# Attention in 24-query blocks with exact maxima, its output kept transposed in SBUF, and a list scheduler in the source

## The chip, the core and the metric

The kernel runs on one core of a Trainium2 chip. Five engines work side by side, each through its own instructions in order: TensorE (PE; its weight loads are listed as PEld), VectorE (DVE), ScalarE (ACT), GpSimd (POOL) and SyncE (SP, which only issues transfers here). Transfers between DRAM and SBUF run on 16 DMA engines; they are issued from SP, ACT or POOL. PE writes into PSUM, eight banks of 128 x 512 float32. The metric is the device time of one execution in microseconds (us), the median of three runs.

## What is computed

For 8 batches of 8 heads, 576 positions, head size 64, two attentions are added. The first pools q, k and v by four along the sequence (144 positions), does a full softmax attention and repeats each output row four times. The second lets each position see only the positions less than four away. The sum, with heads side by side, is a 4608 x 512 input to a gated feed-forward network (FFN) with 1536 inner columns.

```python
factor = 4; Sd = S // factor; scale = 1.0 / np.sqrt(D)
out_up = np.repeat(sm_attn(q_d, k_d, v_d), factor, axis=2)   # q_d, k_d, v_d: means of four
mask = np.abs(pos[:, None] - pos[None, :]) < factor
scores = np.where(mask, scale * np.matmul(q, k.transpose(0, 1, 3, 2)), -1000000000.0)
attn = softmax(scores)                                       # with the row maximum subtracted
attn_out = out_up + np.matmul(attn, v)
x = attn_out.transpose(0, 2, 1, 3).reshape(B * S, H * D)     # 4608 x 512
out = (np.maximum(x @ w_gate, 0.0) * (x @ w_val)) @ w_out    # 512 -> 1536 -> 512
```

## The kernel before

The attention works on 32 pairs of heads (`hp`), four pairs to a batch. The FFN works on nine chunks of 512 tokens; a chunk needs whole batches, since a batch has 576 tokens and all eight heads of it make up the 512 columns of x.

For a pair, `emit_load` brings q and k (96 partitions, six blocks of 96 queries) and windows of v (128 partitions: 96 rows with three before and 29 behind them) into SBUF, all issued from SP. `emit_mid` casts them to float16. `emit_mid_b` transposes q and k on PE against an identity (`tp_ps`, L319), copies them out of PSUM (qT on ACT L328, kT on DVE L330) and pools them by four with two reductions on DVE (L336, L342). `emit_compute` then does the downsampled scores (`sd_ps`, L366), pools v by a matmul with a constant (`vd_ps`, L377), computes band scores in blocks of 96 queries against 128 keys (`sc_ps`, L405), takes exponentials on ACT without subtracting a maximum (L389, L415), multiplies the band by a 0/1 mask on DVE (L418), and sums up: `od_ps` (L429) is the downsampled output with the denominators in a 65th column, `u_ps` (L463) the band output, likewise; `f_ps` (L475) repeats the normalised downsampled output four times by a matmul with a constant. DVE normalises and adds into `x_b` (L484 to L492). Each pair's part of x is written to a DRAM scratch `x_dr` (L503), and transposing loads (L153) bring it back as the `xT` tiles that the FFN needs.

The FFN of a chunk is 12 tasks `ffn_task_h` (L170 and L175: four matmuls each for gate and value, relu on ACT L180, product on DVE L182) and four tasks `ffn_task_y` (12 matmuls each, L191, copied out by ACT L195 and stored). The order is written by hand: the list `sched` gives each pair two slots, and chunk c starts in slot 8c + 11, that is, in the second slot of pair 5 for chunk 0, two tasks to a slot; what has no slot left comes after the last pair (`tail`). Weights arrive in float32 from the ACT queue into staging tiles (L140) and are cast on ACT (L145). Tile pools decide where instructions wait for buffers; PSUM tiles of every kind share the eight banks.

```python
slot = 8 * c + 11
for i, t in enumerate(tasks):
    s = slot + i // 2
    if s < 2 * NP:
        sched[s // 2][s % 2].append(t)
    else:
        tail.append(t)
```

## Time and profile before

| | us |
|---|---|
| median of the three timed runs | 441.45 |
| lowest and highest of them | 439.75, 442.13 |
| span of the profiled execution, first to last instruction | 440.1 |
| PE busy in it | 397.4 |
| DVE busy | 298.4 |
| ACT busy | 211.4 |
| POOL busy | 7.7 |

The profiled execution's time is known by its span alone. A row of the timeline or of the chain of waits starts with the start and the duration in us; matmuls are pipelined, so that their cost is read from start to start and not from the duration. In the groups, `x32 | 23.7, 740` means 32 instructions, 23.7 us busy in all, 740 ns of one; what follows the second bar is idle time of the engine ahead of them and what ended it. `SPq` and `ACTq` are the issuing queues.

### The profile page before, as it was taken

The page shows a single profiled execution, that of the slowest core. Times are in us where ns is not written, and L with a number is a line of the kernel's source. Part 1 is how long each engine was busy: PE and PEld are TensorE (multiplying, and loading weights), DVE is VectorE, ACT ScalarE, POOL GpSimd, SP SyncE. Part 2 cuts the span into 40 slices and gives each one's busy share as a digit, 9 for nine tenths or more (in the row PEclk, how much of TensorE's full clock was granted, in tenths as well). Part 3 has the DMA queues.
Part 4 walks back from the last instruction along what each step waited for, and adds up shares of the span by engine and source line. Part 5 has one row for each costly group of instructions (what it writes and reads, how often), then busy time and mean ns, then how long its engine had stood idle before and what let it go on. Part 6 is the DMA issues. An engine that isn't in the chain of part 4 may idle for free.

```text
span 440.1 us, 9037 instructions
## 1 busy us (share of the span) xinstructions
PE 397.4 (90%) x3408; PEld 227.6 (52%) x3408; DVE 298.4 (68%) x812; ACT 211.4 (48%) x485; POOL 7.7 (2%) x100
## 2 busy tenths in 40 slices
PE   0037778999999999999999999999999999999996
PEld 0026675555555555555565556555655654444442
DVE  0229998998789878977997799779966860330430
ACT  2435876564565455545564556445633532332331
POOL 0000000000000000000000000000000000000000
PEclk9999999999999999999999999999999999999999
DMA  8799989457777787577775646321123112200202
GB/s 288 245 311 224 278 226 243 107 114 174 188 185 172 166 207 176 135 165 215 173 162 132 191 105 138 76 105 33 30 36 109 27 39 48 97 0 9 87 0 95
DMA packets 171730, 60.64 MB, mean 138 GB/s; under 512 B 164264, under 2 KB 164520, under 8 KB 171688
## 3 DMA queue, kind: packets, MB, share of 16 engines
q1 hardware_dynamic: 164008, 41.21, 42.5%
q10 hardware_dynamic: 7680, 18.88, 11.4%
q8 instruction: 26, 0.43, 0.4%
q14 instruction: 16, 0.13, 0.1%
HBM read 41.20 MB, written 14.16 MB: 126 GB/s over the span
## 4 chain that ended last, share of the span: by engine, by line
PE 82%; DMA 7%; DVE 6%; SPq 3%; issue 1%; ACT 1%; DVEq 0%
PE h_ps L170 21%; PE h_ps L175 21%; PE y_ps L191 19%; PE tp_ps L319 3%; PE f_ps L475 3%; PE od_ps L429 3%; PE u_ps L463 3%; DMA vst<-in_v_dram 3%; PE vd_ps L377 3%; PE sc_ps L405 2%; DMA nat<-in_k_dram 2%; SPq L292 2%; PE sd_ps L366 1%; DMA out_dram<-y_sb 1%; DMA masks_sb<-band_masks 1%; SPq L261 1%
## 5 line engine op out<-in xcount | busy, mean ns | idle before, releaser
L170 PE MATMUL h_ps<-xT,wg_sb 128*128 128x512 f16 x432 | 112.1, 382 | 0.0
L175 PE MATMUL h_ps<-xT,wv_sb 128*128 128x512 f16 x432 | 111.7, 381 | 0.0
L191 PE MATMUL y_ps<-wo_sb,gT 128*128 128x512 f16 x432 | 95.7, 379 | 0.0
L175 PEld LDWEIGHTS <-wv_sb 128*128 128x128 f16 x432 | 42.5, 98 | 51.6 <-issue 1.1
L191 PEld LDWEIGHTS <-gT 128*128 128x128 f16 x432 | 41.5, 98 | 48.2
L170 PEld LDWEIGHTS <-wg_sb 128*128 128x128 f16 x432 | 40.3, 99 | 42.3 <-issue 1.6
L195 ACT COPY y_sb<-y_ps 128x512 f32<-128x512 f32 x36 | 21.1, 586 | 78.8 <-PE y_ps L191 72.8
L415 ACT ACTIVATE e_sb<-sc_ps 128x288 f16<-128x288 f32 x128 | 42.0, 416 | 1.1 <-PE sc_ps L405 1.1
L418 DVE TENSOR_TENSOR e_sb<-e_sb,masks_sb 128x288 f16<-128x288 f16 x128 | 36.3, 301 | 4.9 <-ACT e_sb L415 4.9
L463 PEld LDWEIGHTS <-e_sb 128*96 128x96 f16 x384 | 24.8, 138 | 12.0 <-DVE e_sb L418 6.5
L463 PE MATMUL u_ps<-vwin,e_sb 128*96 128x65 f16 x384 | 25.3, 220 | 6.2 <-DVE e_sb L418 6.2
L389 ACT ACTIVATE e_d<-sd_ps 72x288 f16<-72x288 f32 x64 | 22.5, 402 | 16.9 <-PE sd_ps L366 16.8
L394 DVE CAST vd_sb<-vd_ps 72x130 f16<-72x130 f32 x64 | 15.6, 284 | 20.4 <-PE vd_ps L377 20.4
L330 DVE CAST kT<-tp_ps 128x288 f16<-128x288 f32 x64 | 26.7, 442 | 1.5 <-PE tp_ps L319 1.5
L475 PE MATMUL f_ps<-odn,E_sb 72*96 72x64 f16 x384 | 25.6, 220 | 0.0
L429 PE MATMUL od_ps<-vd_sb,e_d 72*72 72x65 f16 x256 | 18.4, 206 | 7.8 <-DVE vd_sb L394 5.9
L328 ACT CAST qT<-tp_ps 128x288 f16<-128x288 f32 x64 | 23.5, 431 | 0.8 <-PE tp_ps L319 0.5
L342 DVE TENSOR_REDUCE k_dT<-kT 128x144 f16<-128x576 f16 x32 | 23.7, 740 | 0.0
L336 DVE TENSOR_REDUCE q_dT<-qT 128x144 f16<-128x576 f16 x32 | 23.6, 739 | 0.0
L475 PEld LDWEIGHTS <-E_sb 72*96 72x96 f16 x384 | 22.8, 138 | 0.0
L307 DVE CAST vwin<-vst 128x768 f16<-128x768 f32 x32 | 17.7, 553 | 6.5 <-DMA vst<-in_v_dram 6.5
L429 PEld LDWEIGHTS <-e_d 72*72 72x72 f16 x256 | 16.9, 123 | 10.0 <-issue 3.8
(556 smaller groups left out, 452.9 us busy)
## 6 DMA issues: line engine op xcount, KB each, us to landing
vst<-in_v_dram SPq DMA_DIRECT2D x62, 192.0 KB
nat<-in_q_dram SPq DMA_DIRECT2D x32, 288.0 KB
nat<-in_k_dram SPq DMA_DIRECT2D x32, 288.0 KB
out_dram<-y_sb ACTq DMA_DIRECT2D x8, 1024.0 KB
x_dr<-x_b SPq DMA_DIRECT2D x32, 144.0 KB
wstage<-in_moe_w_gate_dram ACTq DMA_DIRECT2D x4, 768.0 KB
wstage<-in_moe_w_val_dram ACTq DMA_DIRECT2D x4, 768.0 KB
wstage<-in_moe_w_out_dram ACTq DMA_DIRECT2D x12, 256.0 KB
```

The costliest lines, as they stand in the source:

```text
L170: nc.tensor.matmul(out=h1, lhsT=wg_sb[:, kk, bass.ts(jj, 128)], rhs=xts[kk], start=(kk == 0), stop=(kk == 3),)
L175: nc.tensor.matmul(out=h2, lhsT=wv_sb[:, kk, bass.ts(jj, 128)], rhs=xts[kk], start=(kk == 0), stop=(kk == 3),)
L191: nc.tensor.matmul(out=y_ps, lhsT=st["gts"][jj][:, bass.ts(ty, 128)], rhs=wo_sb[:, jj, :], start=(jj == 0), stop=(jj == NJJ - 1),)
L328: nc.scalar.copy(out=o, in_=tp)
L330: nc.vector.tensor_copy(out=o, in_=tp)
L336: nc.vector.tensor_reduce(out=q_dT, in_=qT[:, KPAD : KPAD + S].rearrange("p (t f) -> p t f", f=4), axis=mybir.AxisListType.X, op=ALU.add,)
L342: nc.vector.tensor_reduce(out=k_dT, in_=kT[:, KPAD : KPAD + S].rearrange("p (t f) -> p t f", f=4), axis=mybir.AxisListType.X, op=ALU.add,)
L415: nc.scalar.activation(out=esb, in_=scps[hh][:, :, 0:NQ], func=AF.Exp, scale=scale)
L418: nc.vector.tensor_tensor(out=esb, in0=esb, in1=masks_sb[:, 3 * g2 : 3 * g2 + 3, :], op=ALU.mult,)
L429: nc.tensor.matmul(out=od_ps[0:72, hh, tcx, :], lhsT=ed_sb[hh][:, c, bass.ts(tcx, 72)], rhs=vd_sb[hh][:, c, :], start=(c == 0), stop=(c == 1),
L463: nc.tensor.matmul(out=up[:, j, :], lhsT=e_sb[hh][j // 3][:, j % 3, :], rhs=vw[:, hh, j, :], start=True, stop=True,)
L475: nc.tensor.matmul(out=fp[:, j, :], lhsT=E_sb[0:72, j % 3, :], rhs=odn_sb[hh][0:72, j // 3, :], start=True, stop=True,)
```

## The change

The attention is written anew, the FFN keeps its matmuls, and the whole program is put in order by a planner in the source: every piece of work is an `Op` with an engine (or several to choose from), an assumed duration, the ops it depends on and a priority; `list_schedule` simulates five in-order engines, takes at each step the op that can start first (among those within 0.05 us, the one of the lowest priority number), and the instructions are emitted in that order. Attention has lower numbers than the FFN. PSUM's banks are split, four for the FFN and four for attention.

For a pair, q and k come as nine tiles of 128 rows with both heads side by side (`nat`), are cast (`c16`), and nine PE transposes (T) give q and k of both heads as one `qkT`. One reduction pools both by four (`qkd`). The scores (S) are computed with queries on the partitions: 24 blocks of 24 queries against 32 keys for each of two heads, 48 matmuls with 32-column weights of 64 rows, and 12 matmuls of 24 downsampled queries against 144 keys. DVE adds a mask of 0 and -1e30, takes row maxima, subtracts them, and after the exponential on ACT sums, inverts and normalises; the downsampled maxima go by POOL (scaled by `nb`) into the bias of three exponentials on ACT. The band weights are transposed in 32 x 32 blocks on DVE (`at2`), the downsampled ones on PE (W, six transposes) and copied by ACT. V multiplies: 12 matmuls for the band, 4 for the downsampled part, with the output transposed (head columns on the partitions). v is loaded twice, as windows (`vw32`) and in groups of four rows (`v4`) that are added up by POOL or DVE. Two additions on DVE write the sum, downsampled columns repeated by the access pattern, straight into `xT` in SBUF; the DRAM scratch, its writes and transposing loads, the staging tiles and casts of the weights are gone. The weights are loaded by POOL's queue with the cast to float16 done by the transfer. Stores of y go from SP, one for each 128 tokens.

```diff
-    sched = [[[], []] for _ in range(NP)]
...
-            vd = a_vd.tile([72, 2, 65], FP16, name="vd_sb", tag="vd_sb")
...
-        nc.sync.dma_start(
-            _dap(
-                x_dr,
...
+    def start_of(o, eng):
+        t = max(avail[eng], data_at(o, eng))
+        if o.need:
+            name, n = o.need
+            p = pools[name]
+            if len(p) < n:
+                return None
+            t = max(t, sorted(p)[n - 1][0] + SEM)
+        return t
+
...
+        best = None
+        starts = {}
+        ends = {}
+        for e, rs in ready.items():
+            for o, dur in rs:
+                s = start_of(o, e)
+                if s is None:
+                    continue
+                starts[o.seq, e] = s
+                ends[o.seq] = min(ends.get(o.seq, (1e9, "")), (s + dur, e))
+        for (i, e), s in starts.items():
+            if ends[i][1] == e and (best is None or s < best[0]):
+                best = (s, e)
+        assert best is not None, "the graph is stuck"
+        t0, e = best
+        o, dur = min(((o, d) for o, d in ready[e]
+                      if starts.get((o.seq, e), 1e9) <= t0 + eps[e] and ends[o.seq][1] == e),
+                     key=lambda x: (x[0].prio, x[0].seq))
...
+    for g in range(4):
+        for nm, dst, src in (("g", wg_sb, moe_w_gate), ("v", wv_sb, moe_w_val)):
+            w_ld[nm, g] = add(POOL, 1.2, wpiece(dst, src, 384 * g, 384, 0), prio=-40 + g,
+                              xfer=2.2, after=6.0 + 5.0 * g)
+    for g in range(4):
+        w_ld["o", g] = add(POOL, 1.2, wopiece(3 * g, 3), prio=-30 + g, xfer=2.2,
+                           after=28.0 + 3.0 * g)
...
+        r["cast"] = cast = add_any(
+            copies(c_, nt_, (POOL, 1.15), (DVE, 0.77), (ACT, 1.2)),
+            [lq, lm, lm2, lk, before2.get("T")], prio=P + 10)
+
+        def emit_T(o):
+            for t in range(9):
+                bk = bank[o.banks[0 if t < 5 else 1]].bitcast(FP16)
+                col = 128 * (t if t < 5 else t - 5)
+                nc.tensor.transpose(bk[:, col : col + 128], c_[:, t, :], ident)
+        r["T"] = T = add(PE, 0.55, emit_T, [cast, ld_id], prio=P + 11, need=("A", 2), key=("T", p))
...
+        pl = add(DVE, 1.35, emit_pool, [ev1, ev2, before3.get("S")], prio=P + 14)
+
+        def emit_S(o):
+            sc, sp = bank[o.banks[0]], bank[o.banks[1]]
+            scv = sc[:, 0:384].rearrange("p (i j) -> p i j", j=32)
+            for i in range(12):
+                for par in range(2):
+                    blk = 2 * i + par
+                    for hh in range(2):
+                        c = 2 * par + hh
+                        nc.tensor.matmul(
+                            out=scv[32 * c : 32 * c + 32, i, :],
+                            lhsT=qk_[64 * hh : 64 * hh + 64, 24 * blk : 24 * blk + 32],
+                            rhs=qk_[64 * hh : 64 * hh + 64, S + 24 * blk - 3 : S + 24 * blk + 29],
+                            start=True, stop=True)
+            spv = sp[:, 0 : 3 * SD].rearrange("p (i j) -> p i j", j=SD)
+            for i in range(3):
+                for par in range(2):
+                    g = 2 * i + par
+                    for hh in range(2):
+                        c = 2 * hh + par
+                        nc.tensor.matmul(
+                            out=spv[32 * c : 32 * c + 32, i, :],
+                            lhsT=qkd[S3][64 * hh : 64 * hh + 64, 24 * g : 24 * g + 32],
+                            rhs=qkd[S3][64 * hh : 64 * hh + 64, SD : 2 * SD],
+                            start=True, stop=True)
+        r["S"] = Sx = add(PE, 1.6, emit_S, [pl], prio=P + 20, need=("A", 2), key=("S", p))
...
+        msk = add(DVE, 0.56, lambda o: nc.vector.tensor_tensor(
+            out=s_, in0=bank[Sx.banks[0]][:, 0:384].rearrange("p (i j) -> p i j", j=32),
+            in1=mask_sb, op=ALU.add), [Sx, ld_mask, before3.get("exp")], prio=P + 21)
+        dmax = add(DVE, 0.60, lambda o: nc.vector.tensor_reduce(
+            out=nmx[S3][:, 0:3], in_=bank[Sx.banks[1]][:, 0 : 3 * SD].rearrange(
+                "p (i j) -> p i j", j=SD), axis=AX.X, op=ALU.max, negate=True),
+            [Sx, before3.get("nrd")], prio=P + 22)
+        nb = add(POOL, 0.15, lambda o: nc.gpsimd.tensor_scalar(
+            out=nmb[S3][:, 0:3], in0=nmx[S3][:, 0:3], scalar1=scale / 16.0, scalar2=None,
+            op0=ALU.mult), [dmax], prio=P + 22.5)
+        mxo = add(DVE, 0.56, lambda o: nc.vector.tensor_reduce(
+            out=mx[S3], in_=s_, axis=AX.X, op=ALU.max), [msk], prio=P + 23)
+        sub = add_any(either(lambda e: e.tensor_tensor(
+            out=s_, in0=s_, in1=bc12(mx[S3]), op=ALU.subtract), (POOL, 0.90), (DVE, 0.56)),
+            [mxo], prio=P + 24)
+        r["exp"] = ex = add(ACT, 0.52, lambda o: nc.scalar.activation(
+            out=e_, in_=s_, func=AF.Exp, scale=scale),
+            [sub, *[before3.get(n) for n in ("tr0", "tr1")]], prio=P + 25)
+        smo = add(DVE, 0.56, lambda o: nc.vector.tensor_reduce(
+            out=sm[S3], in_=e_, axis=AX.X, op=ALU.add), [ex], prio=P + 26)
+        rco = add(DVE, 0.18, lambda o: nc.vector.reciprocal(out=rs[S3], in_=sm[S3]),
+                  [smo], prio=P + 27)
+        nrm = add_any(either(lambda e: e.tensor_tensor(
+            out=e_, in0=e_, in1=bc12(rs[S3]), op=ALU.mult), (POOL, 0.90), (DVE, 0.56)),
+            [rco], prio=P + 28)
+        tr = []
+        for par in range(2):
+            lo = 64 * par
+            tr.append(add(DVE, 0.56, lambda o, lo=lo: nc.vector.transpose(
+                out=at2[S3][lo : lo + 64, :, lo // 2 : lo // 2 + 32], in_=e_[lo : lo + 64]),
+                [nrm, z_at[S3], before3.get("V")], prio=P + 29))
+            r[f"tr{par}"] = tr[-1]
...
+        exd = []
+        for i in range(3):
+            exd.append(add(ACT, 0.45, lambda o, i=i: nc.scalar.activation(
+                out=wd_[:, i, :], in_=bank[Sx.banks[1]][:, SD * i : SD * i + SD], func=AF.Exp,
+                bias=nmb[S3][:, i : i + 1], scale=scale / 16.0,
+                accum_out=smd[S3][:, i : i + 1]),
+                [nb, before2.get("W")], prio=P + 24 + 0.1 * i,
+                free=[("S", p)] if i == 2 else ()))
+        for a, b2 in zip(exd, exd[1:]):
+            b2.deps.append(a)
+        exd[-1].deps.append(msk)
+        rcd = add(DVE, 0.18, lambda o: nc.vector.reciprocal(
+            out=rsd[S3][:, 0:3], in_=smd[S3][:, 0:3]), exd, prio=P + 27.5)
+        r["nrd"] = nrd = add_any(either(lambda e: e.tensor_tensor(
+            out=wd_, in0=wd_, in1=_sap(rsd[S3], 0, 128, 0, [[1, 3], [0, SD]]), op=ALU.mult),
+            (POOL, 1.0), (DVE, 0.61)), [rcd], prio=P + 28.5)
...
+        def emit_W(o):
+            bk = bank[o.banks[0]].bitcast(FP16)
+            for kc in range(2):
+                for i in range(3):
+                    n = 3 * kc + i
+                    nc.tensor.transpose(bk[0:72, 128 * n : 128 * n + 128],
+                                        wd_[:, i, 72 * kc : 72 * kc + 72], ident)
+        r["W"] = W = add(PE, 0.36, emit_W, [nrd], prio=P + 30, need=("A", 1), key=("W", p))
...
+        r["vcast"] = vc = add_any(copies(
+            vw16[S3], vw_, (POOL, 1.4), (DVE, 0.97), (ACT, 1.5)), lv + [before3.get("V")], prio=P + 26)
...
+        r["vs"] = vso = add_any(either(lambda e: e.tensor_tensor(
+            out=vs[S2], in0=v4_[:, :, 0:128], in1=v4_[:, :, 128:256], op=ALU.add),
+            (POOL, 1.2), (DVE, 0.69)),
+            [l4, before2.get("vd")], prio=P + 26.2)
+        r["vd"] = vdo = add_any(either(lambda e: e.tensor_tensor(
+            out=_sap(vdz[S3], 0, 72, 0, [[320, 2], [128, 2], [1, 64]]),
+            in0=vs[S2].rearrange("p (h c) e -> p h c e", h=2)[:, :, :, 0:64],
+            in1=vs[S2].rearrange("p (h c) e -> p h c e", h=2)[:, :, :, 64:128], op=ALU.add),
+            (POOL, 0.65), (DVE, 0.43)), [vso, z_vd[S3], before3.get("V")], prio=P + 26.3)
...
+        def emit_V(o):
+            for i in range(12):
+                bk = bank[o.banks[i // 6]]
+                col = 48 * (i % 6)
+                nc.tensor.matmul(
+                    out=bk[:, col : col + 48], lhsT=vw16[S3][:, i, :],
+                    rhs=at2[S3][:, i, :].rearrange("p (a c) -> p a c", c=32)[:, :, 0:24],
+                    start=True, stop=True)
+            od = bank[o.banks[0]][:, 288 : 288 + SD]
+            n = 0
+            for hh in range(2):
+                for kc in range(2):
+                    nc.tensor.matmul(
+                        out=od, lhsT=vdz[S3][:, hh, kc, :],
+                        rhs=wT[S2][:, 3 * kc : 3 * kc + 3, hh],
+                        start=(n == 0), stop=(n == 3))
+                    n += 1
+        r["V"] = V = add(PE, 0.95, emit_V, [*tr, vc, vdo, evw], prio=P + 40, need=("A", 2),
+                         key=("V", p))
+        odc = add(ACT, 0.29, lambda o: nc.scalar.mul(
+            out=od_sb[S2], in_=bank[V.banks[0]][:, 288 : 288 + SD], mul=0.25),
+            [V, before2.get("xa")], prio=P + 41)
+        xa = []
+        for half in range(2):
+            def emit(o, half=half):
+                t0 = b * S + 288 * half
+                nc.vector.tensor_tensor(
+                    out=xT[:, kk, t0 : t0 + 288].rearrange("p (t f) -> p t f", f=4),
+                    in0=bank[V.banks[half]][:, 0:288].rearrange("p (t f) -> p t f", f=4),
+                    in1=_sap(od_sb[S2], 0, 128, 72 * half, [[1, 72], [0, 4]]), op=ALU.add)
+            xa.append(add(DVE, 0.45, emit, [odc] + xa, prio=P + 42 + half,
...
+        xdeps = [x_add[bb, kk, hf] for bb, hf in halves for kk in range(4)]
...
+            h1 = add(PE, 0.862, lambda o, f=emit_h: f(o, wg_sb), xdeps + [w_ld["g", g]],
+                     prio=fprio, need=("F", 1), key=("h1", c, jj))
...
+            rl = add(ACT, 0.60, lambda o, h1=h1, rt=rt: nc.scalar.activation(
+                out=rt, in_=bank[h1.banks[0]], func=AF.Relu),
+                [h1, r1_last.get(n_h % 4)], prio=-10, free=[("h1", c, jj)])
+            gslot = 12 * (c % 2) + jj
+            gm = add(DVE, 0.67, lambda o, h2=h2, rt=rt, gslot=gslot: nc.vector.tensor_tensor(
+                out=gT[gslot], in0=rt, in1=bank[h2.banks[0]], op=ALU.mult),
+                [rl, h2, *[y_last.get((c - 2, ty)) for ty in range(4)]], prio=-10,
+                free=[("h2", c, jj)])
...
+    order = list_schedule(ops, {"F": [0, 1, 2, 3], "A": [4, 5, 6, 7]},
+                          {PE: 0.05, ACT: 0.05, DVE: 0.05, POOL: 0.05, SP: 0.05})
+    with tc.manual_schedule():
+        for o in order:
+            o.emit(o)
```

## The prediction

> **What bounds the kernel now.** First the totals: the busy table and, under it, PE's busy tenths in the forty slices of the span.

> ```profile
> span 440.1 us, 9037 instructions
> PE 397.4 (90%) x3408; PEld 227.6 (52%) x3408; DVE 298.4 (68%) x812; ACT 211.4 (48%) x485; POOL 7.7 (2%) x100
> PE   0037778999999999999999999999999999999996
> ```

> PE is full from the seventh slice on; before that it is not. So I asked for stretches: start, fill, two of the steady state.

> ```profile
> 12.80:34.00 21.20, 4.66 (x51) 3.66 (x51) 6.48 (x19) 7.88 (x15) 0.00 (x0) 1.00 0.90 270
> 34.00:72.00 38.00, 29.17 (x352) 26.35 (x353) 36.59 (x115) 28.41 (x65) 1.29 (x18) 1.00 1.00 235
> 105.00:192.60 87.60, 87.46 (x819) 49.98 (x816) 73.97 (x207) 46.55 (x116) 2.00 (x24) 1.00 0.76 181
> ```

> Columns: PE, PEld, DVE, ACT, POOL, granted clock, DMA share, GB/s. Up to 34 us the transfers set the pace (DMA 0.90), from 34 to 72 DVE does (36.6 of 38), afterwards PE (87.46 of 87.60), with DVE at 84%. The chain of waits, in order of time, gives the edges; the next three rows are the timeline.

> ```profile
> 71.97 1.71 PE h_ps L170 x4
> 80.44 0.86 PE h_ps L170 x4
> 105.06 5.18 PE y_ps L191 x24
> 148.87 5.18 PE y_ps L191 x24
> 192.59 5.18 PE y_ps L191 x24
> ```

> ```profile
> 425.80 10.52 PE L191 MATMUL y_ps<-wo_sb,gT 128*128 128x512 f16 x48
> 436.36 0.59 ACT L195 COPY y_sb<-y_ps 128x512 f32<-128x512 f32 x1 [2.00 <-DMA out_dram<-y_sb]
> 436.97 0.34 ACTq L197 DMA_DIRECT2D out_dram<-y_sb  x1
> ```

> A group of four FFN matmuls takes 5.18/6 = 0.8635 us. There are 1296/4 = 324 groups: 280 us that no order changes. A chunk (36 groups, four pairs of heads) repeats every 43.76 us (the mean of two), so attention costs PE (43.76 - 31.09)/4 = 3.17 us a pair. The first group takes 1.71 us instead of 0.86 although the granted clock reads 1.00: until about 75 us PE runs at half rate. Account: 72 (first FFN) + 2 (half-rate groups) + 280 + 26 pairs x 3.17 = 82 makes 436, and 4 more pass from the last matmul (425.80 + 48 x 0.216 = 436.2) to the end, copy, issue and landing: 440. The median of the timed runs, 441.45, stands 1.35 above this span; I add 1.35 at the end.

> So the change can win in two terms: the 72 us before the first FFN group, and PE's price of the pairs behind it. It must not let DVE become the bound.

> **The change, part by part.** *Moved and removed.* The round trip of x through DRAM (32 writes, 36 transposing loads) goes; it lay beside other transfers and hid behind the two pairs that before's order puts between a batch and its chunk, so I count it only in the fill. Before's six kinds of small matmul become T, S, W and V. New waits: W on PE waits for exponentials that wait for a maximum scaled on POOL; FFN groups stand behind it on PE, and relu and products behind those. *Order.* In the built order, PE issues ahead of the first FFN group 6 transposes (T), 6 score groups (S), and 4 each of W and V; between there and the last V 169 FFN groups, 26 T, 26 S, 28 W, 28 V; then 155 FFN groups alone. In that last stage each two groups (1.73 us) need one relu and one product, as in the tail of before, where PE never waits: 155 x 0.8635 = 133.8 us, plus the 4 behind the last matmul.

> *PE's price of a pair, at full rate.* T is 9 transposes of 128 columns, W 6; V is 12 matmuls of 48 columns and 4 of 144; S is 48 of 32 columns with 32-column weights, and 12 of 144 columns. The timeline of a steady pair has the nearest rows:

> ```profile
> 133.66 0.68 PE L319 MATMUL tp_ps<-I_sb,qk_2197 96*128 96x96 f16 x12
> 134.17 1.03 PE L170 MATMUL h_ps<-xT,wg_sb 128*128 128x512 f16 x4
> 137.63 0.69 PE L463 MATMUL u_ps<-vwin,e_sb 128*96 128x65 f16 x12
> 138.15 0.70 PE L475 MATMUL f_ps<-odn,E_sb 72*96 72x64 f16 x12
> 141.28 1.03 PE L175 MATMUL h_ps<-xT,wv_sb 128*128 128x512 f16 x4
> 142.24 0.32 PE L366 MATMUL sd_ps<-q_dT,k_dT 64*72 64x144 f16 x4
> 142.49 0.54 PE L377 MATMUL vd_ps<-vwin,p_sb 128*72 128x130 f16 x6
> 142.96 0.43 PE L405 MATMUL sc_ps<-qT,kT 64*128 64x96 f16 x12
> 143.41 0.29 PE L429 MATMUL od_ps<-vd_sb,e_d 72*72 72x65 f16 x4
> 143.54 0.25 PE L319 MATMUL tp_ps<-I_sb,qk_2407 96*128 96x96 f16 x2
> ```

> Start to start: tp 0.51 us for 1152 columns, so T (1152) 0.50 and W (768) 0.34. u 0.52 for 12, sd 0.25 for 4 of 144 columns: V 0.77. Entering S costs the gap ahead of sd (141.28 + 0.864 to 142.24): 0.1. S itself has no row. Upper end: od's 0.13/4 = 32 ns for each of the 48, sd's 62 ns for each of the 12: 2.3 us. Lower end: by columns (0.44 ns each in tp) 14 ns, and 31 ns where two row halves run side by side: 1.05. The sc row alternates row halves as S does and takes 37 ns for 96 columns, which by columns would be 42: nearly no overlap. So I stay near the upper end: 28 and 55 ns, 2.0 us. A pair costs 0.50 + 0.34 + 0.77 + 0.1 + 2.0 = 3.7 us instead of 3.17. PE in the mixed stage: 169 x 0.8635 = 145.9, plus 26 x 2.6 = 67.6, plus 28 x 1.11 = 31.1: 244.6 us.

> [...]

> *DVE in the mixed stage.* Its built order has 418 instructions between the first FFN product and the last addition into xT: 60 products, 26 poolings, 26 mask additions, 80 reductions (26 maxima, 26 downsampled maxima, 28 sums), 20 subtractions, 56 reciprocals, 38 normalisations (27 of 384 elements, 11 of 432), 56 block transposes, 56 additions. Durations, the spacing of two neighbours, and a handoff from ACT (total, times, longest) from:

> ```profile
> L342 DVE TENSOR_REDUCE k_dT<-kT 128x144 f16<-128x576 f16 x32 | 23.7, 740 | 0.0
> L330 DVE CAST kT<-tp_ps 128x288 f16<-128x288 f32 x64 | 26.7, 442 | 1.5 <-PE tp_ps L319 1.5
> L484 DVE RECIPROCAL rdu<-u_ps 96x6 f32<-96x6 f32 x64 | 9.0, 172 | 12.6 <-PE u_ps L463 12.1
> L182 DVE TENSOR_TENSOR gT<-r_4025,h_ps 128x512 f16<-128x512 f16 x1 | 0.7, 690 | 0.3 <-PE h_ps L175 0.3
> 49.77 0.74 DVE L336 TENSOR_REDUCE q_dT<-qT 128x144 f16<-128x576 f16 x1
> 50.43 0.74 DVE L342 TENSOR_REDUCE k_dT<-kT 128x144 f16<-128x576 f16 x1
> DVE e_sb L418 <- ACT e_sb L415: 4.9, 21, 0.5
> ```

> Within 20 ns they fit 145 ns plus 1.04 ns an element: pooling (1152) 1.34, mask, maximum, sum, subtraction, normalisation, transpose (384) 0.545, downsampled maximum (432) 0.59, its normalisation 0.595, addition (288) 0.44, product 0.69, reciprocal 0.17. Summed over the order: 232 us. The two reductions of the timeline start 0.66 apart at 0.74 each: neighbours overlap by 0.08, which some 278 of the 418 can do; the other 140 (five a pair) need the instruction just before them. 232 - 22 + 140 x 0.05 = 217 us. For the 0.05 the ends are 0 and the 4.9/21 = 0.23 us that DVE waits for ACT; I take a value near the low end because nothing crosses to another engine. Below PE's 245, so PE bounds, with 3 us for handoffs missed. ACT's 304 instructions there are far below (170 us by the same method).

> *The fill.* Removed: six 0.8 KB pieces and the weights in front of pair 0's v; added: v arrives as windows and once more in fours, 11 issues a pair on SP, weights cast in flight from POOL behind twelve memsets.

> ```profile
> 9.45 0.51 ACT L301 CAST qk_153<-nat 96x384 f16<-96x384 f32 x1 [0.54 <-DMA nat<-in_q_dram]
> 21.34 0.56 DVE L307 CAST vwin<-vst 128x768 f16<-128x768 f32 x1 [5.80 <-DMA vst<-in_v_dram]
> 3.03 0.47 SPq L261 DMA_DIRECT2D nat<-in_q_dram  x1
> 36.68 0.46 PE L366 MATMUL sd_ps<-q_dT,k_dT 64*72 64x144 f16 x4 [0.58 <-DVE k_dT L342]
> 37.07 0.86 PE L377 MATMUL vd_ps<-vwin,p_sb 128*72 128x130 f16 x6
> 39.43 0.40 PE L429 MATMUL od_ps<-vd_sb,e_d 72*72 72x65 f16 x4 [0.74 <-DVE vd_sb L394]
> 39.64 0.43 PE L319 MATMUL tp_ps<-I_sb,qk_373 96*128 96x96 f16 x3
> ```

> Eight issues of some 0.47 us put pair 0's q and k (0.58 MB) on the way by 4.5 us; at the 235 to 270 GB/s above they are in by 6.5. Cast 1.2, T 0.9, two copies 1.3, pool 1.35: the first S starts at 11.3. At half rate sd takes 97 ns and od 52 ns apiece (last four rows), 1.6 times the warm price, so an S costs 3.3 us, W 0.6, V 1.4. Followed through the built order by hand, PE and DVE take turns: S1 waits for the pool that stands behind pair 0's subtraction, V0 for W0 behind S1, and each pair then advances in about 8.5 us, of which PE is busy 6.2. 11.3 + 3.3 for the first S; xa of pair 3 some 36 us of DVE work and 5 of waits later, at 55; S of pairs 4 and 5 stand ahead of the first FFN group on PE's queue, and end at 58. Bounds: 50 (S at its lower end) and 72 (no gain). Loads behind these waits on SP go three pairs ahead and cost nothing while they land; without that cover each pair's 1.25 MB costs about 5 us.

> *Sum:* 58 + 2 + 245 + 3 + 134 + 4 = 446, plus 1.35: **447 us**, 1.3% above the median. Beside the account of before: the first FFN group comes 14 us earlier, but behind it stand 98.7 us of attention on PE (67.6 + 31.1) instead of 82, and 3 us of missed handoffs. Own range: the fill moves it by 8 either way, S between 1.6 and 2.3 by -10 and +8; added in squares, 434 to 458.

> **The rivals.** *Small matmuls are cheap (faster).* With S at 1.3 us the PE mixed stage is 226, the six S of the fill lose 1.1 us each at half rate (51), and DVE at 217 stands so close that I give 6 more: 51 + 2 + 232 + 134 + 4 + 1.35 = **424 us**. For it: 32-column weights are shorter than any in the trace. Against it: sc. It decides once S is below about 1.7. [...]

> *DVE becomes the bound (slower).* 58 DVE instructions of the mixed stage (20 subtractions, 38 normalisations) read two SBUF tensors while POOL, now with some 135 casts and sums of its own instead of

> ```profile
> L306 POOL MEMSET vwin<- 128x12 f16 x32 | 4.7, 153 | 305.7 <-PE u_ps L463 162.0 <-issue 136.5 <-DVE kT L330 6.9
> ```

> is at work. If each is held for one 384-element instruction (0.47 us spaced), that is 27 us; if the 140 dependent neighbours cost the 0.23 us of an ACT handoff rather than 0.05, 25 more: 217 + 52 = 269, and the total 58 + 2 + 269 + 134 + 4 + 1.35 = **468 us**. It decides from 28 us of such delay. Nothing in before shows POOL beside DVE. [...]

> *The start is not shortened.* Four weight pieces stand on POOL's in-order queue behind work that waits for pair 0's maximum; if they hold chunk 0's products until before's 72: 447 + 14 = **461 us**. Against it: 6.3 MB of weights and four pairs' 5.0 MB take 45 us at 250 GB/s.

> **How the numbers follow.** Forecast 0.48, cheap matmuls 0.28, DVE bound 0.17, late start 0.07. Of the forecast's 0.48 the lower part of its own range falls within 0.5% of before (2.2 us, about what a measurement can tell from no change), 0.11, and 0.03 below that. Faster 0.31, same 0.11, slower 0.34 + 0.17 + 0.07 = 0.58. The range takes in both outer cases but their ends: 424 to 469.

> **What would show it.** First FFN matmul at 58 us (50: cheap S; 72: late start). S, start to start, 2.0 us warm. Between first FFN group and last V 248 us with PE over 97% busy; DVE busy there about 217 to 232. If PE has idle time ahead of W and V while DVE is full, DVE is the bound. If DVE's two-input instructions last longer than 0.55 us, POOL holds them. I am wrong if the first FFN group comes after 66 us or S costs under 1.6.

## The result and the profile after

The changed kernel takes 464.65 us (median, 462.8 to 465.2) where the kernel before takes 440.6 beside it (439.26 to 442.13): the ratio is 1.0525, with a 95% interval of 1.0486 to 1.0564. The forecast was 447 us. It is slower, as forecast, but by 24 us instead of 6.

The page of the changed kernel, its totals and three of the rows of forty slices (busy tenths of PE and DVE, granted clock):

```profile
span 463.4 us, 10721 instructions
PE 374.4 (81%) x4208; PEld 196.5 (42%) x4208; DVE 315.8 (68%) x547; ACT 212.3 (46%) x509; POOL 180.3 (39%) x195
PE   1124339876787987988879998899999999999996
DVE  4178668967989999999999999999133132230330
PEclk9999999998979999899989999999999999999999
```

PE is busy for 374 us instead of 397, in a span that is 23 us longer. PE's unbroken nines begin only at the 27th slice; in slices 13 to 28 it is DVE that shows nothing but nines, and behind them it shows no more than three. The same in stretches: the two halves of the fill, then from the first FFN matmul to the end of the last attention matmul (the mixed stage), then the FFN alone. Columns as in the prediction.

```profile
0.00:34.00 34.00, 5.56 (x144) 3.95 (x144) 15.42 (x27) 8.71 (x15) 16.85 (x27) 1.00 0.93 172
34.00:72.00 38.00, 15.56 (x360) 12.09 (x358) 28.36 (x50) 13.95 (x37) 19.41 (x20) 1.00 1.13 196
72.06:326.04 253.98, 219.42 (x3091) 120.02 (x3088) 238.09 (x422) 148.99 (x388) 143.97 (x148) 0.97 0.66 147
326.04:459.86 133.82, 133.82 (x621) 60.46 (x618) 33.85 (x50) 40.09 (x68) 0.00 (x0) 1.00 0.10 38
```

| part (us) | forecast | measured |
|---|---|---|
| before the first FFN matmul | 58 | 72.06 |
| mixed stage: PE at work | 2 + 245 | 219.42 |
| mixed stage: PE idle | 3 | 34.56 |
| FFN alone | 134 | 133.82 |
| behind the last matmul | 4 | 3.54 |
| median less span | 1.35 | 1.25 |
| sum | 447 | 464.65 |

Three terms are wrong, and two of them nearly cancel: PE has 28 us less work in the mixed stage than forecast, and 32 us more idle time. What is left of the miss is the fill's 14 us and 4 from these two. The other terms are together 0.7 us below the forecast. The rest of the reading asks where the three come from.

*The fill.* The chain of waits in order of time (start, length, what), and DVE's timeline:

```profile
16.26 9.76 DMA vw<-in_v_dram
38.08 7.75 DMA vw<-in_v_dram
```

```profile
26.14 0.96 DVE L251 CAST vw<-vw 128x1536 f16<-128x1536 f32 x1 [11.82 <-DMA vw<-in_v_dram]
27.02 0.55 DVE L412 TENSOR_TENSOR s_sb<-bank,mask_sb 128x384 f32<-128x384 f32 x1
```

A cast of v's windows stands in DVE's order ahead of a pair's mask, and DVE waits 11.82 us for its data; the mask starts only behind it. Over the fill the DMA engines are full (0.93 and 1.13), and DVE, busy 36.6 of 38 us there before, is busy 28.36: the fill is bound by transfers. The view shows 172 and 196 GB/s, where the forecast stood on 235 to 270, but these figures do not compare. The queues of the first 72 us (packets, MB, share of all engines' time), before and then after:

```profile
q1 hardware_dynamic: 35328, 9.03, 59.4%
q10 hardware_dynamic: 2880, 9.44, 35.6%
q1 hardware_dynamic: 28862, 8.49, 60.5%
q0 software_dynamic: 5824, 4.72, 42.6%
```

The second row of each is the weights. Before, they land as float32, 9.44 MB; after, the transfer casts them, and the view counts the 4.72 MB that land. Counted as DRAM holds them, the changed kernel's two queues moved 17.9 MB in 72 us, 249 GB/s, and before's 18.5. The rate was the forecast's; there was more to move than it counted, and weights and pairs' blocks share the engines from the start.

*PE's work.* The warm timeline of PE, with a T, a V, two pairs' S and a W:

```profile
200.03 0.67 PE L360 MATMUL bank<-ident_sb,c 128*128 128x128 f16 x9
200.53 1.03 PE L579 MATMUL bank<-xT,wv_sb 128*128 128x512 f16 x4
...
202.25 0.46 PE L527 MATMUL bank<-at,vw 128*128 128x48 f16 x12
202.56 0.41 PE L535 MATMUL bank<-wT,vdz 72*128 72x144 f16 x4
202.90 0.52 PE L388 MATMUL bank<-qkT 64*32 64x32 f16 x48
203.25 0.38 PE L399 MATMUL bank<-qkd 64*32 64x144 f16 x12
203.56 1.04 PE L579 MATMUL bank<-xT,wv_sb 128*128 128x512 f16 x4
205.27 0.52 PE L388 MATMUL bank<-qkT 64*32 64x32 f16 x48 [0.68 <-DVE xT L549]
...
212.08 0.53 PE L469 MATMUL bank<-ident_sb,wd 128*72 128x128 f16 x6
212.44 1.03 PE L579 MATMUL bank<-xT,wg_sb 128*128 128x512 f16 x4
```

Start to start, S takes 203.56 - 202.90 = 0.66 us: 0.35 for the 48 matmuls of 32 columns, 7.3 ns each, and 0.31 for the 12 of 144 columns. The forecast had 2.0. V takes 0.65 here, forecast 0.77; T 0.50, as forecast, and W 0.36, forecast 0.34. By before's rows, one of the 48 would take 14 ns (32 columns at tp's 0.44) and one of the 12, as in sd, 62; at 7.3 and 26 ns (0.31/12) they overlap.

*PE's idle time.* The second S shows its form: PE waits, in order, for a step of attention. What PE waited for most in the mixed stage (total, times, longest), and DVE's groups with two SBUF inputs, over the whole span:

```profile
PE bank L388 <- DVE xT L549: 5.5, 6, 1.6
PE bank L360 <- ACT wd L449: 5.0, 6, 2.1
PE bank L399 <- DVE qkd L375: 4.7, 5, 1.3
```

No wait stands out: the whole list has 34 us in 37 waits, of which DVE ended 19 us, ACT 10 and POOL 4.

```profile
L434 DVE TENSOR_TENSOR e<-e,rs 128x384 f16<-128x384 f16 x31 | 25.2, 814 | 0.5
L424 DVE TENSOR_TENSOR s_sb<-s_sb,mx 128x384 f32<-128x384 f32 x24 | 24.0, 1001 | 0.8
L412 DVE TENSOR_TENSOR s_sb<-bank,mask_sb 128x384 f32<-128x384 f32 x32 | 17.7, 553 | 0.5
L460 DVE TENSOR_TENSOR wd<-wd,rsd 128x432 f16<-128x432 f16 x15 | 16.3, 1086 | 0.4
```

L412, of the same 384 elements but with one input in PSUM, takes 553 ns (forecast 545); L434 and L424, with both inputs in SBUF, take 814 and 1001, and L460 1086 instead of 595. So two explanations for the idle time stood side by side: DVE, slowed in this way, bounds the mixed stage; or the order laid out by the scheduler gives PE too little to do between the steps of attention. The experiments tell them apart.

### The profile page after: what moved, and what is told of

Same layout as the page of the kernel before. It is cut to its first block, busy times and chain, and to the rows that moved or that the text cites. A ratio compares the mean times of both kernels' runs of the same rounds, so it can differ in the third digit from the quotient of the medians.

```text
span 463.4 us, 10721 instructions
## 1 busy us (share of the span) xinstructions
PE 374.4 (81%) x4208; PEld 196.5 (42%) x4208; DVE 315.8 (68%) x547; ACT 212.3 (46%) x509; POOL 180.3 (39%) x195
## 3 DMA queue, kind: packets, MB, share of 16 engines
q0 software_dynamic: 5824, 4.72, 6.6%
HBM read 50.46 MB, written 9.44 MB: 129 GB/s over the span
## 4 chain that ended last, share of the span: by engine, by line
PE 43%; DVE 28%; SPq 10%; DMA 8%; issue 6%; POOL 3%; ACT 2%; DVEq 0%; POOLq 0%; ACTq 0%
PE bank L579 25%; PE bank L605 15%; DVE qkd L375 5%; DVE gT L591 5%; DMA vw<-in_v_dram 4%; SPq L336 4%; SPq L499 3%; DVE at L440 3%; DMA v<-in_v_dram 3%; DVE xT L549 3%; SPq L341 2%; DVE e L434 2%; DVE s_sb L424 2%; DVE wd L460 2%; DVE s_sb L412 2%
## 5 line engine op out<-in xcount | busy, mean ns | idle before, releaser
L591 DVE TENSOR_TENSOR gT<-r,bank 128x512 f16<-128x512 f16 x108 | 73.6, 681 | 95.3 <-PE bank L579 90.9
L579 PE MATMUL bank<-xT,wv_sb 128*128 128x512 f16 x432 | 112.5, 383 | 0.0
L579 PE MATMUL bank<-xT,wg_sb 128*128 128x512 f16 x432 | 112.0, 382 | 0.0
L605 PE MATMUL bank<-wo_sb,gT 128*128 128x512 f16 x432 | 104.0, 393 | 0.1
L587 ACT ACTIVATE r<-bank 128x512 f16<-128x512 f32 x108 | 64.6, 598 | 70.6 <-PE bank L579 70.2
L360 PE MATMUL bank<-ident_sb,c 128*128 128x128 f16 x288 | 26.1, 242 | 34.2 <-ACT c L249 20.5
L512 POOL TENSOR_TENSOR vs<-v 72x512 f32<-72x512 f32 x31 | 41.7, 1346 | 10.8 <-DMA v<-in_v_dram 8.9
L375 DVE TENSOR_REDUCE qkd<-qkT 128x288 f16<-128x1152 f16 x32 | 42.9, 1344 | 1.8 <-ACT qkT L249 1.6
L251 POOL CAST vw<-vw 128x1536 f16<-128x1536 f32 x27 | 40.4, 1497 | 9.5 <-DMA vw<-in_v_dram 7.6
L249 ACT COPY qkT<-bank 128x640 f16<-128x640 f16 (+1 forms) x62 | 37.5, 645 | 14.4 <-PE bank L360 13.5
L440 DVE STREAM_TRANSPOSE at<-e 64x384 f16<-64x384 f16 x64 | 36.5, 571 | 1.2
L251 POOL CAST c<-nat 128x1152 f16<-128x1152 f32 x21 | 24.9, 1188 | 27.3 <-PE bank L360 12.1
L469 PE MATMUL bank<-ident_sb,wd 128*72 128x128 f16 x192 | 17.9, 235 | 18.9 <-DVE wd L460 9.0
L419 POOL TENSOR_SCALAR nmb<-nmx 128x3 f32<-128x3 f32 x32 | 8.3, 260 | 57.5 <-DVE nmx L415 53.9
L460 POOL TENSOR_TENSOR wd<-wd,rsd 128x432 f16<-128x432 f16 x17 | 18.7, 1103 | 22.6 <-DVE rsd L458 11.2
```

The source lines that it names most:

```text
L249: return lambda o: nc.scalar.copy(out=dst, in_=src(o) if callable(src) else src)
L251: return lambda o: e.tensor_copy(out=dst, in_=src(o) if callable(src) else src)
L360: nc.tensor.transpose(bk[:, col : col + 128], c_[:, t, :], ident)
L375: nc.vector.tensor_reduce(out=qkd[S3], in_=qk_[:, 0:1152].rearrange("p (t f) -> p t f", f=4), axis=AX.X, op=ALU.add)
L440: tr.append(add(DVE, 0.56, lambda o, lo=lo: nc.vector.transpose(out=at2[S3][lo : lo + 64, :, lo // 2 : lo // 2 + 32], in_=e_[lo : lo + 64] ...
L512: r["vs"] = vso = add_any(either(lambda e: e.tensor_tensor(out=vs[S2], in0=v4_[:, :, 0:128], in1=v4_[:, :, 128:256], op=ALU.add), (POOL, 1 ...
```

## The experiments

All of them change the changed kernel ("after" in the table). The table gives, for each, the first FFN matmul, then for the stretch from there to the end of the last attention matmul its length, PE's busy and idle time and DVE's busy time, then the FFN alone, and the time. Stretches come from one profiled execution. Idle is length less busy, and since PE's busy time counts modelled tails it is a little low, for all runs alike. Busy time includes what half-rate clock adds. The first five have one time each, so their times are known to a few microseconds at best; the kernel before took 443.15 beside the first four and 440.8 to 441.5 beside the others.

| run (us) | first FFN | mixed | PE busy | PE idle | DVE busy | FFN alone | time |
|---|---|---|---|---|---|---|---|
| before | 71.8 | 285.1 | 283.7 | 1.4 | 234.4 | 79.4 | 440.6 |
| after | 72.1 | 254.0 | 219.4 | 34.6 | 238.1 | 133.8 | 464.65 |
| e1 one SBUF input | 70.9 | 240.0 | 214.5 | 25.5 | 216.8 | 133.8 | 450.05 |
| e2 weights late | 60.5 | 262.7 | 228.2 | 34.5 | 239.2 | 127.8 | 456.52 |
| e3 no v in fours | 68.8 | 255.8 | 227.2 | 28.6 | 242.4 | 120.9 | 452.0 |
| e4 no maxima | 60.8 | 225.6 | 187.3 | 38.3 | 194.6 | 164.9 | 456.68 |
| e5 POOL memsets | 72.2 | 233.1 | 211.7 | 21.3 | 217.1 | 133.8 | 444.46 |
| e6 FFN between pairs | 72.7 | 297.2 | 275.9 | 21.3 | 274.7 | 69.9 | 447.43 |
| e7 = e6 + e1 + e2 | 60.7 | 303.7 | 275.6 | 28.1 | 259.5 | 71.7 | 441.78 |
| e8 = e7 + all durations | 60.5 | 287.8 | 278.6 | 9.1 | 258.7 | 67.3 | 422.62 |
| e9 durations of PE, transfers | 68.6 | 271.6 | 259.9 | 11.7 | 255.7 | 87.2 | 433.05 |
| e10 = e7 + durations of PE | 67.8 | 290.9 | 273.2 | 17.7 | 249.7 | 68.2 | 429.57 |
| e11 = e7 + durations of POOL, ACT, DVE | 77.1 | 290.5 | 275.6 | 14.9 | 256.4 | 68.2 | 443.98 |
| e12 = e6 + all durations | 68.2 | 284.8 | 277.7 | 7.1 | 253.8 | 69.1 | 428.24 |
| e13 durations of transfers | 66.3 | 256.9 | 229.8 | 27.2 | 246.3 | 118.3 | 450.5 |
| e14 = e9 + e1 | 65.9 | 265.8 | 257.3 | 8.5 | 234.6 | 87.2 | 425.75 |
| e15 = e8, FFN a pair sooner | 57.5 | 307.9 | 290.9 | 16.9 | 261.9 | 64.8 | 435.55 |
| e16 = e8, weights at 20 and 45 us | 60.2 | 283.8 | 276.6 | 7.2 | 255.2 | 67.3 | 416.57 |

### Does POOL hold DVE's two-input instructions?

**e1** puts the maxima and reciprocals into free PSUM columns where the instruction that reads them runs on DVE; order and counts stay.

```diff
+    mxp = [bank[4][:, 440 + 12 * i : 452 + 12 * i] for i in range(3)]
+    def at(user, near, far):
+        return near if user.eng == DVE else far
-            out=s_, in0=s_, in1=bc12(mx[S3]), op=ALU.subtract)
+            out=s_, in0=s_, in1=bc12(at(sub, mxp[S3], mx[S3])), op=ALU.subtract)
...
```

> Changed kernel, same order on every engine; where DVE subtracts the maximum or normalises, the 12 (or 3) maxima or reciprocals lie in free columns of a PSUM bank, so that these 70 instructions read one SBUF tensor instead of two. Theory 'POOL holds them': their means fall from 814, 1001 and 1086 ns to 550 to 600, DVE's work in the mixed stage shrinks by some 22 us, and the time falls from 463 towards 445 (less where a PSUM bank is waited for). Rival 'they are slow by themselves' (broadcast input, dependence on the instruction before): the means stay, the time stays at 463.

DVE's groups in that run (the lines stand 7 or 8 further down):

```profile
L442 DVE TENSOR_TENSOR e<-e,bank 128x384 f16<-128x384 f16 x31 | 17.1, 553 | 1.2 <-PE bank L406 0.7
L431 DVE TENSOR_TENSOR s_sb<-s_sb,bank 128x384 f32<-128x384 f32 x24 | 13.3, 553 | 6.1 <-ACT wd L457 2.5 <-ACT wT L481 1.4 <-PE bank L543 0.8
L468 DVE TENSOR_TENSOR wd<-wd,bank 128x432 f16<-128x432 f16 x15 | 9.0, 602 | 1.1 <-PE bank L406 0.7
```

814, 1001 and 1086 ns become 553, 553 and 602 with one operand moved. DVE's busy time in the mixed stage falls from 238.1 to 216.8 us, where the forecast had 217, and the stage shortens by 14.0. PE still idles for 25.5.

**e5** leaves DVE as it was and lets POOL write without reading: its casts of loaded blocks and its sums of v are replaced by memsets of the same destinations.

```diff
-            return lambda o: e.tensor_copy(out=dst, in_=src(o) if callable(src) else src)
+            if eng == POOL:
+                return lambda o: nc.gpsimd.memset(dst[:], 0.0)
+            return lambda o: nc.vector.tensor_copy(out=dst, in_=src(o) if callable(src) else src)
...
```

> In this run POOL's casts of the loaded blocks and its sums of v are replaced by memsets of the same destinations, so POOL is busy in the same places but reads no SBUF there (its normalisations and the scaled maxima still read; DVE's work is as in the changed kernel). Theory (a two-input DVE instruction waits for a POOL instruction that reads SBUF, not for any POOL instruction): DVE's normalisation of 384 and its subtraction fall from 814 and 1001 ns to 0.56 to 0.65 us. Rival (any busy POOL holds them): they stay at 0.75 to 1.0 us. Second rival (POOL's writes hold them): they fall only as far as the memsets are shorter than the casts. Time about 450 us by the theory, 460 to 465 by the rival.

```profile
L435 DVE TENSOR_TENSOR e<-e,rs 128x384 f16<-128x384 f16 x31 | 18.2, 586 | 0.5
L425 DVE TENSOR_TENSOR s_sb<-s_sb,mx 128x384 f32<-128x384 f32 x24 | 13.4, 558 | 0.8
L461 DVE TENSOR_TENSOR wd<-wd,rsd 128x432 f16<-128x432 f16 x15 | 9.4, 629 | 0.4
```

These DVE groups read the same two SBUF tensors as in the changed kernel and take 586, 558 and 629 ns. So what holds them here is POOL's casts and sums, which read SBUF, and not its memsets, which only write. The changed kernel has both cases: the normalisation (L434) at 79.89 us, with POOL idle, takes 0.56 us, and the one at 110.29, beside a cast of v on POOL (110.39, 1.46 us), 1.97. POOL's own work was shorter too (131 us instead of 180), so the 20 us by which this run is faster are not all due to DVE. Both runs keep the order and the planned durations of the changed kernel, and PE's idle time falls all the same, from 34.6 us to 25.5 and 21.3: by e1, 9 us of it came from these instructions; e5's 13 include what POOL's shorter work gave. Together the two runs show that the 814, 1001 and 1086 ns take both: a second SBUF input on DVE (553, 553 and 602 ns without it) and the casts and sums on POOL (586, 558 and 629 with memsets in their place).

### What sets the fill?

**e2** lets the scheduler issue the weight pieces later, **e3** leaves out the loads of v in fours behind the third pair (what is summed from them is stale).

```diff
-                              xfer=2.2, after=6.0 + 5.0 * g)
+                              xfer=2.2, after=30.0 + 4.0 * g)
-                           after=28.0 + 3.0 * g)
+                           after=60.0 + 3.0 * g)
```

```diff
-        l4 = add(SP, 0.4, lambda
+        l4 = None if p >= 3 else add(SP, 0.4, lambda
```

> Changed kernel with the planner's earliest times of the weight transfers moved: gate and value from 6 us on to 30 us on, output weights from 28 to 60. Theory 'transfers hold the fill': the windows of v of pair 1, which landed at 26.1 us, land at about 16; the first FFN matmul comes at 58 to 64 us instead of 72, the time falls to 450 to 456. Rival 'the chain of PE, DVE and ACT holds it': first FFN matmul at 70 to 74, time within 2 us of 463.

> Changed kernel that leaves out the second load of v (rows in fours) from the fourth pair on; the sums of four are then taken of old data. It has 0.29 MB less of 1.25 MB to load for each of these pairs. Theory 'transfers hold the fill': first FFN matmul 4 to 7 us earlier, time 456 to 460. Rival 'the chain': first FFN matmul at 70 to 74.

With the weights out of the way the first FFN matmul comes at 60.5 instead of 72.1, close to the 58 of the forecast. Its fill from 20 to 40 us:

```profile
20.00:40.00 20.00, 9.71 (x251) 7.72 (x251) 17.00 (x28) 9.55 (x25) 12.80 (x13) 1.00 1.02 194
```

The DMA engines are as full as in the changed kernel, but by 60 us only 1.86 MB of the weights have landed. So the 11.6 us came from what is transferred first. Only 8 us of it reached the time: the mixed stage grew by 8.7 (PE was busy for 228.2 us in place of 219.4, with a mean clock of 0.94), and 6 came back from a shorter stage of FFN alone. e3 moved the first FFN matmul by 3 us, less than the theory's 4 to 7, and the time by some 12, more than its theory had, most of it because 15 more FFN groups fit into a mixed stage that is hardly longer.

### Does a lighter DVE help?

**e4** takes work from DVE instead of waits: both maxima and the subtraction are left out, and the exponentials have no bias, so the output is that of a softmax without its maxima.

```diff
-        nb = add(POOL, 0.15, lambda
+        nb = None if True else add(POOL, 0.15, lambda
-        mxo = add(DVE, 0.56, lambda
+        mxo = None if True else add(DVE, 0.56, lambda
-        sub = add_any(either(
+        sub = msk if True else add_any(either(
...
```

> Changed kernel that leaves out the maxima of both attentions and their subtraction (the exponentials are taken of the masked scores), so also POOL's scaling of the downsampled maximum. In the mixed stage DVE loses 15 + 17 + 20 = 52 us of its 238. Theory 'DVE bounds the mixed stage': PE, with 220 us at most, bounds instead; the stage shrinks from 254 to 215 to 225 us and the time falls to 425 to 435. Rival 'PE waits for handoffs of the written order whatever DVE does': the stage shrinks by less than 20 us.

The time missed by 20 us and more, though the mixed stage has nearly the length that the theory gave it:

```profile
60.80:286.40 225.60, 187.32 (x3016) 107.08 (x3013) 194.60 (x355) 136.20 (x367) 119.59 (x109) 0.95 0.82 169
```

DVE has 43 us less to do and the mixed stage is 28 us shorter, but PE idles for 38 us all the same, and the scheduler, planning anew, left 31 us more of FFN for the end. Whatever makes PE idle, a full DVE is not all of it; with a new plan the run cannot say how much.

### Is it the order?

**e6** keeps every instruction and changes the priorities of the FFN groups alone: each chunk's groups lie among the pairs that follow it, not behind all attention. **e7** adds the edits of e1 and e2, and **e8** sets the scheduler's durations close to those that the profile of the changed kernel shows.

```diff
-            fprio = FP + 1000 * c + 10 * jj
+            fprio = 100 * (4 * c + 4 + 2.0 + 8 * jj / 36)
...
-                    prio=FP + 1000 * c + 125 + 3 * ty + part, **kw))
+                    prio=100 * (4 * c + 4 + 2.0 + 4 * (24 + 3 * ty + part) / 36), **kw))
```

```diff
-        r["T"] = T = add(PE, 0.55, emit_T,
+        r["T"] = T = add(PE, 0.50, emit_T,
-        r["S"] = Sx = add(PE, 1.6, emit_S,
+        r["S"] = Sx = add(PE, 0.75, emit_S,
-        r["W"] = W = add(PE, 0.36, emit_W,
+        r["W"] = W = add(PE, 0.34, emit_W,
-        r["V"] = V = add(PE, 0.95, emit_V,
+        r["V"] = V = add(PE, 0.60, emit_V,
...
-            copies(c_, nt_, (POOL, 1.15), (DVE, 0.77), (ACT, 1.2)),
+            copies(c_, nt_, (POOL, 1.19), (DVE, 0.77), (ACT, 1.15)),
...
-        lq = add(SP, 1.0, load(nt_, 0, 128, 0, 4, q, 0), w, prio=P, xfer=0.6)
+        lq = add(SP, 1.0, load(nt_, 0, 128, 0, 4, q, 0), w, prio=P, xfer=0.9)
...
```

> In this run the FFN's priorities in the scheduler lie between those of the pairs (each chunk's groups spread over the pairs that follow it) instead of behind all attention; the instructions are the same ones. Theory (PE's 41 us of idle time behind the first FFN group come from attention taken first: attention runs at the pace of DVE and the transfers with PE waiting in order, and 134 us of FFN alone remain in which DVE has nothing to do): first FFN group at 72 us as before, idle time of PE behind it falls to 5 to 15 us, FFN alone at the end about 70 us, time 425 to 435 us. Rival (the idle time is made by the handoffs of the small matmuls, wherever they stand): idle stays near 40 us and the time at 455 to 465.

> This run has three edits at once: the FFN spread between the pairs, the weight pieces asked for later, and the maxima and reciprocals in PSUM so that DVE's three kinds of two-input instruction have one SBUF input. Theory: the gains add, since they lie in different stages: first FFN group at 60 us, then 347 us of PE work and 5 to 10 of idle, 4 behind the last matmul: 416 to 423 us, below both kernels. Rival (the fill and the idle time share one cause, the transfers, so the gains overlap): 430 to 440 us.

> As the run with the three edits, but the scheduler's durations are set to those measured in the profile of the changed kernel (the small matmuls shorter, POOL's casts and sums longer, the transfers longer). Theory (the planned order was wrong mainly through the attention-first priority, hardly through durations): 412 to 423 us, within 5 us of the run before. Rival (wrong durations made the order): more than 10 us faster than the run with the three edits.

e6 gains 17 us but keeps 21 us of idle time, between its theory and its rival. e7 misses both its theory (416 to 423) and its rival (430 to 440): the three gains do not add, PE idles for 28 us, and its ratio to before is 1.0035 (1.0005 to 1.0065). Then e8, with the same steps as e7 and only the numbers changed that the scheduler plans with (so that some steps go to other engines), takes 19 us less: 0.9581 (0.9545 to 0.9617). Its rival was right: here the durations matter more than the priority.

**e9** puts that to the test in the changed kernel itself, with attention first and the slow two-input instructions left in: only PE's four durations and the transfers' are corrected. **e13** corrects the transfers' alone. **e10** and **e11** split the correction from e7 to e8: PE's durations, or those of POOL, ACT and DVE. **e12** is e8 without the edits of e1 and e2.

> The changed kernel with nothing altered but two kinds of the scheduler's durations: the four small-matmul steps of a pair on PE (0.55, 1.6, 0.36 and 0.95 us become 0.50, 0.75, 0.34 and 0.60) and the transfers (half as long again). Attention stays ahead of the FFN in priority, the two-input instructions stay. Theory (the planner believed that a pair costs PE 3.46 us where it costs 2.1, so it laid too few FFN groups between the pairs, and PE idles for about the difference, 28 times 1.4 = 39 us): the FFN alone at the end shrinks from 155 groups to 101, PE's idle time behind the first FFN group falls from 41 us to 10 to 25, time 440 to 450. Rival (the priority of attention makes the idle time, whatever the durations): idle 30 to 45 us, 452 to 466.

> As the run with the three edits (441.8 us), and of the durations only the four of PE's small-matmul steps corrected. Theory (the overstated price of the small matmuls was what cost that run its last 19 us): 422 to 429 us. Rival (POOL's and the transfers' durations were what counted): 436 to 442.

> As the run with the three edits (441.8 us), and of the durations only those of POOL, ACT and DVE corrected (casts, sums, scaled maxima, normalisations). Theory (PE's durations count): 436 to 442 us. Rival (POOL's count): 422 to 429.

> FFN between the pairs and all durations corrected, but the weight pieces asked for as early as in the changed kernel and the maxima and reciprocals in SBUF. Against the run with everything (422.6 us) it lacks those two edits. Theory (the two are worth what they were worth alone where their stage still bounds: the fill 11 us; the two-input instructions less than the 14 us of before, as DVE has slack once the FFN is spread): 434 to 440 us, first FFN group at 72 us and idle time behind it 8 to 14 us. Rival (DVE held by POOL bounds the spread order too): 445 to 450.

> The changed kernel with only the transfers' durations corrected; PE's small-matmul steps keep their 3.46 us a pair. Theory (the overstated price on PE makes the idle time): 137 groups stand behind the last attention instead of 155, PE's idle time behind the first FFN group stays at 28 to 38 us, 450 to 460 us. Rival (the transfers' durations do it): idle at 10 to 18 us, 433 to 440.

The mixed stage of e9:

```profile
68.63:340.19 271.56, 259.88 (x3376) 140.55 (x3373) 255.71 (x446) 160.60 (x408) 147.90 (x154) 0.99 0.66 147
```

e9 takes 433.05 us, better than its theory's 440 to 450: 0.9816 of before (0.9761 to 0.9871). Ten constants of a plan, and the change is faster, by a little less than 2%, than the kernel that it replaced. PE idles for 11.7 us, and 101 groups are left for the end instead of 155. DVE does about the same work per pair, slow instructions included (71 of them in place of 70), in a longer stage. e13 stays at 450.5 with 27 us of idle time, so the step from there to e9, 17 us, is PE's durations; the transfers' gave the other 14 of the 32, through a fill 6 us shorter (with one T and one S fewer ahead of the first FFN matmul) and 7 us less idle time. The same from the other base: e10 gains 12 us on e7, e11 nothing (443.98 against 441.78, with a first FFN matmul at 77 us). What makes up the 7 us from e10 to e8 was not tried. e12 takes 428.24, less than its theory: with the right durations the first FFN matmul comes at 68.2 without the weights being moved.

The reason stands in the source. The scheduler believed that a pair costs PE 0.55 + 1.6 + 0.36 + 0.95 = 3.46 us. By the rows of PE's work above it costs 0.50 + 0.66 + 0.36 + 0.65 = 2.17. Over some 28 pairs of the mixed stage that is 36 us in which the plan has PE at work and the chip has it free, to wait for the next step of its list or to run ahead. That 34.6 us of idle time were measured beside these 36 is in part luck: with the same 3.46 us in the plan PE idles for 25.5 us in e1, 21.3 in e5 and 27.2 in e13. The corrected plan also moves other instructions, so how much of the gain is the number of groups between the pairs was not tried by itself.

### What is left once the order is right?

**e14** adds the edit of e1 to e9. **e15** and **e16** vary e8: the FFN's priorities one pair earlier (the 2.0 above becomes 1.0), or the weight pieces asked for at 20 and 45 us.

> As the run with PE's and the transfers' durations corrected (433 us), and the maxima and reciprocals in PSUM. Theory (with the order right DVE has slack, so the two-input instructions no longer set the time): 430 to 434 us. Rival (they are still worth the 14 us that they were worth in the changed kernel): 418 to 423.

> As the run with everything (422.6 us), with the FFN groups' priorities one pair earlier. Theory (PE has 8 us of idle time behind the first FFN group, and the fill is set by the transfers of the pairs, not by priorities): 420 to 425 us. Rival (the groups wait behind later pairs' steps): 414 to 419.

> As the run with everything (422.6 us), with the weight pieces asked for at 20 and 45 us instead of 30 and 60. Theory (the pairs' loads and the weights share the same 190 GB/s, so earlier weights delay the loads by as much as they come sooner): first FFN group at 60 to 65 us, 422 to 427 us. Rival (the first FFN groups wait for their weights): first group before 58 us, under 420.

e14 takes 425.75 us, 7.3 less than e9: the two-input instructions are worth half of the 14.6 that e1 showed, between theory and rival. e15, outside both its theory and its rival, is slower than e8 by 13 though its first FFN matmul comes 3 us earlier: PE idles 8 us more and is busy 10 longer, and the last section shows what the latter comes from. e16 is the fastest: 416.57 us, 0.9449 of before (0.9399 to 0.9499). Its first FFN matmul is where e8's is and where its theory had it, but the time is below the theory's 422 to 427 and fits the rival's, whose reason, an earlier first FFN matmul, did not come; its 6 us over e8 are spread (2 idle, 2 busy, the rest within the spread of single executions), and why was not pursued. So one small change of a plan can move the time by 6 or 13 us for reasons that nobody foresaw, and a single step of that size, like e10's 12, proves little by itself; that e9, e8, e10 and e12 all point the same way carries more. e16's row of PE, and the clock, of which no fall is recorded:

```profile
PE   0341459999999999999998999999998999999996
PEclk9999999999999999999999999999999999999999
```

## Why the prediction was right and wrong

- **The start of the list (58 us): wrong, 72.06.** This is most of the miss of 17.65 us. The step that failed is the one that let loads "cost nothing while they land". The chain started as forecast, with the first S at 11.30 us (forecast 11.3), but PE then idles 8.26 us ahead of pair 1's T and 6.03 us inside its S, for q, k and v that come late. The rate was not it: 249 GB/s in the fill, counted as DRAM holds the data. The sum against the late start, 45 us for 11.3 MB, took two thirds of the weights and four pairs; ahead of the first FFN matmul the queues moved 17.9 MB, all the weights and almost seven pairs, which at that rate is the 72 us. e2 gives the size of the collision with the weights, 11.6 us. The forecast had it as a rival, with another holder: POOL's order, not the transfers.
- **S at 2.0 us: wrong, 0.66.** The lower bound, 1.05, was still too high. The choice by the sc row failed: those matmuls alternate two row halves and take 37 ns each, while S, in the source, also writes to four groups of 32 partitions in turn and takes 7.3 and 26 ns; no row of before has that form. The rival "small matmuls are cheap" had the direction right, though its 1.3 is still twice the measured size.
- **Its 424 us, and the forecast's 3 us of idle time: wrong.** Cheap matmuls did not make the stage shorter, they made PE wait, 34.6 us. This is the step that the forecast left out: it summed an engine's work and took the order as given, and did not set S beside the 1.6 us that the order was planned with. At its own 3.7 us a pair the plan's 3.46 would have fitted, so the 3 us of idle time stood and fell with S. The order was visible, 169 groups in the mixed stage and 155 behind, laid out for an S of 1.6 us; the chip followed it with an S of 0.66.
- **DVE at 217 us: right by itself** (216.8 in e1), but 238.1 in the changed kernel. The rival's delay is real: 27 x (841 - 545) + 21 x (959 - 545) + 11 x (1140 - 595) ns = 22.7 us from the mixed stage's rows,

```profile
L434 DVE TENSOR_TENSOR e<-e,rs 128x384 f16<-128x384 f16 x27 | 22.7, 841 | 0.4
L424 DVE TENSOR_TENSOR s_sb<-s_sb,mx 128x384 f32<-128x384 f32 x21 | 20.1, 959 | 0.7
L460 DVE TENSOR_TENSOR wd<-wd,rsd 128x432 f16<-128x432 f16 x11 | 12.5, 1140 | 0.3
```

  where it said 27 for 58 instructions. Its other 25 us, for dependent neighbours, did not come: DVE idles 15.9 us in the whole stage, where 140 handoffs of 0.23 us would be 32. That its 468 us lie near the 464.65 measured is luck, with a fill 14 us too short and a mixed stage 15 us too long. Against a PE that needs 219 us, not 245, DVE's 238 does bound the stage in part (the 14 us of e1); e9, with the slow instructions left in, shows that it is not the main thing.
- **The mixed stage at 250 us: 254.0, right for wrong reasons,** as the table at the start shows. **FFN alone at 134 us and 4 behind it: right** (133.8 and 3.5). That PE would be busy for over 97% of the mixed stage was the test that failed: 86%. (A slip that nothing rests on: before has seven kinds of small matmul, not six.)

## What to carry over

A list scheduler's durations are part of the kernel. On engines that run in order, a step planned too long does not end early for anybody: its engine waits, and work that could have filled the gap stands at the end. So before summing an engine's instructions, set the plan's durations beside the rows, and after the first profile put the measured ones back in; here that was worth 32 us of 465 with no step of the computation changed. A view's GB/s counts what lands (4.72 MB here for 9.44 in DRAM), so set bytes beside bytes where a transfer casts. And do not add up gains from runs whose order was planned anew: e4, e7 and e15 each moved work from one place and met it in another.
